# A build-time scheduler with another model of its DMA queues: DeltaNet followed by a gated MoE layer

## The chip, the cores and the metric

One core of one Trainium2 chip. The metric is the device time of a run in microseconds (us). The engines are called PE (matrix multiply), DVE (VectorE), ACT (ScalarE), POOL (GpSimd) and SP (SyncE, which issues most transfers). PE's weight loads are a row of their own, PEld.

## The reference

Inputs: q, k, v of shape (4 batches, 8 heads, 768 steps, 48), beta (4, 8, 768), w_in (384, 2048), w_out (2048, 384). q, k, v and beta are float32; the kernel gets w_in and w_out as float64 bit patterns.

```python
k_n = k / (norm(k, axis=-1) + 1e-6)
for t in range(768):                       # per batch and head
    y[t] = q[t] @ state                    # state: 48 x 48, from zero
    v_old = state.T @ k_n[t]
    state = state + beta[t] * outer(k_n[t], v[t] - v_old)
x = y.transpose(0, 2, 1, 3).reshape(3072, 384)
h = x @ w_in
out = (h * cos(h)) @ w_out                 # (3072, 384)
```

## The kernel before, in words

**Attention.** The 768 steps are cut into 24 units of 32 steps; the work of one unit covers all 4 batches and 8 heads. Two units are a pair. For unit n the tasks are, in the kernel's own names: loads of `k`, `q`, `v` (four transfers each, one for each batch; from unit 8 on other layouts with more transfers); `turn` (transposes on PE) and `turn_out` (copy by ACT); `gram` (products of keys with keys and queries: 32 small matmuls in the program, 64 in the trace, where every fp32 matmul counts twice); `gram_keys` and `gram_queries` (DVE); `gram_put` (store of the scaled products to DRAM). For each pair, `gram_get` reads them back in another layout, `inv` inverts 128 triangular 32 x 32 matrices column by column (L672 and L679; the first pair on DVE, all later ones on POOL), `put` stores the inverse to DRAM (L688) and `get` reads it back as `zt` (L697). Then, unit after unit: `state` (products with the running state, L714), `right` (DVE), `solve` (L745), `solve_out` (which makes `u`, DVE), `update` (L768) and `update_out` (new state, DVE), `within` (L785), `within_out` (copy of `y`, ACT), `features` (transpose, L804) and `features_out` (`x_ffn`, ACT). The state makes this a chain from unit to unit.

**MoE.** It runs per pair (256 tokens). The first two pairs have plain `hidden` blocks, 8 for each pair (L825, 24 matmuls in the trace), each followed by four steps of gating (`turns` ACT, `rest` DVE, `cos` ACT, `gate` DVE); the first pair also has plain output, 8 `out` groups of 8 matmuls (L970). All other products are Strassen-like: `layer` (L944), `left` and `right` sums on DVE, `product` (L1027) and `collect` (L1077). PSUM has three banks for hidden blocks (tag `h`), and one tile each for most attention products.

**Weights.** 28 `weights` tasks load 64-bit words (0 to 11 are w_in, 12 to 27 w_out) into one of eight shared tiles with the tag `g`. Each then passes `split` (two instructions on ACT), `shift` (two on DVE) and `add` (one on POOL, L488), which leave a float32 weight.

**Order.** Nothing of the order is left to the runtime. The class `Order` holds each of these tasks with an engine, a cost, a due time, what it needs and the buffers that it makes and frees. At build time `run` plays the tasks through a model of the engines: at each moment an engine takes the ready task with the earliest due time whose buffers fit; `NUDGE` shifts due times by kind of task, `STICK` keeps PE with tiles of one size, `stall` adds waits for PE's instruction blocks. The order in which the tasks are emitted is then pinned on each engine. A task that issues transfers is on SP here; in the model its transfers start when one of `IN_FLIGHT = 8` places is free. Each transfer also uses one of eight completion semaphores in turn, over all issuing engines, and the program makes the issuing engine wait for the transfer eight places ahead.

```python
end = max(end, flights[-self.IN_FLIGHT]) + self.ISSUE
dma_free = max(dma_free, end + 0.5) + moves / parts
flights.append(dma_free + 1.4)
```

On the chip each engine runs its own pinned list, and waits for semaphores where the data asks for it. The lists decide what stands behind a waiting instruction.

Of the kernel before, what the change touches and what calls it, by code (L numbers as in the profile page):

```python
# [46 lines left out]
class Order:  # L47
# [9 lines left out]
    WINDOW = 818.445  # L57
    LAG = {"PE": 0.2, "DVE": 0.15, "ACT": 0.15, "POOL": 0.2, "SP": 2.0, "IN": 0.0}
    IN_FLIGHT, ISSUE = 8, 0.49

    STEADY, LATE = 130.0, {"SP": 3.0, "POOL": 2.0}
    SLOW, WARM = 1.7, 4.0
    STICK = 1.823
    CHANGE = 0.15

    EARLY, NUDGE = 6, {('state', True): -3.4, ('features', False): -48.4, ('left', True): 37.6, ('solve', True): -19.7, ('turn', False): 12.2, ('within', True): -6.1, ('features_out', True): 39.0, ('rest', False): -12.6, ('weigh', False): -49.2, ('gram_put', True): 12.6, ('collect', False): -26.2, ('within', False): -32.5, ('features', True): -14.4, ('gate', True): -24.7, ('layer_out', False): -12.4, ('update', True): -10.5, ('sum', False): 24.3, ('layer', False): -1.8, ('add', True): -24.4, ('cos', True): 15.7, ('update', False): -6.1, ('solve', False): -34.1, ('norms', True): -9.2, ('state', False): -9.6, ('sum', True): 20.5, ('right', True): 24.7, ('hidden', True): 17.1, ('blocks', False): 2.6, ('gram', False): -8.1, ('inv_out', False): -15.0, ('v', False): 17.4, ('out', True): -13.0, ('eye', True): -0.5, ('features_out', False): -17.0, ('within_out', False): -0.6, ('gram_get', False): 12.2, ('gram_get', True): -21.0, ('turns', True): 8.1, ('scale', True): 5.8, ('k', True): -20.2, ('shift', True): -4.8, ('shift', False): 2.4, ('collect', True): 0.5, ('out', False): 0.3, ('scale', False): -1.8, ('out_out', True): 0.9, ('weigh', True): 5.0, ('store', True): -5.1, ('split', False): 9.0, ('within_out', True): -1.7, ('turns', False): -10.9, ('store_right', True): 3.6, ('turn_out', True): 1.5, ('k', False): 0.9, ('store_right', False): -5.1, ('inv', False): 5.4, ('square', False): 7.4, ('square', True): 4.1, ('norms', False): -1.3, ('store', False): 3.3, ('hidden', False): -4.1, ('cos', False): 3.4, ('x_sum', False): -0.6, ('beta_home', False): -1.9, ('store_left', True): -3.3, ('get', False): -6.1, ('get', True): 4.0, ('in_sums', False): 2.9, ('gram_queries', True): 1.6, ('turn_out', False): 5.0, ('update_out', False): -0.3, ('store_left', False): 0.1, ('inv', True): 1.1, ('v', True): -0.9, ('eye', False): -2.2, ('x_sum', True): 0.7, ('split', True): -3.1, ('beta_home', True): -4.7, ('weights', True): -0.3, ('gate', False): -3.7, ('put', False): -1.3, ('inv_out', True): -1.1, ('gram_keys', True): 0.6, ('solve_out', False): -1.5, ('add', False): 1.0, ('in_sums', True): 0.3}
# [19 lines left out]
    def add(  # L86
        self, key, engine, cost, emit, deps=(), makes=(), uses=(), moves=0.0, due=1e9
    ):

        assert key not in self.tasks, key  # L90
        self.tasks[key] = [engine, cost, due, emit, set(deps), makes, uses, moves]
        for t in uses:
            self.users[t] = self.users.get(t, 0) + 1
        for tag, t in makes:
            self.tiles[t] = tag
# [7 lines left out]

    def stall(self, key, now, commit):

        n = count = self.count(key)
# [3 lines left out]
        for i in range(self.written + 1, self.written + n + 1):  # L110
            t = now + cost * (i - self.written) / n + stall
            if (i + self.PHASE + self.AHEAD) % self.BLOCK == 0:
                there[(i + self.PHASE + self.AHEAD) // self.BLOCK + 1] = t + self.FETCH
# [135 lines left out]
def kernel(  # L249
# [32 lines left out]
    nc = tc.nc  # L282
# [1204 lines left out]
```

## Time and profile before

| what | before |
|---|---|
| three runs | 670.65, 673.01, 675.20 us; median 673.01 |
| the profiled execution | 673.73 us, its span 672.0 us |
| PE busy | 611.2 us (91% of the span), 11864 matmuls |
| DVE, POOL, ACT busy | 476.5, 347.1, 246.6 us |
| moved by DMA | 52.55 MB, of it 49.98 MB through SP's queue and 0.39 MB through ACT's |

The span runs from the first to the last instruction; the profiled execution's own time is 1.7 us longer. "Busy" rows with forty digits are the span in slices of 16.8 us, each digit a tenth. In a timeline, a line has start, length, engine, source line and operation; brackets tell how long the engine was idle ahead of it and who ended the wait. PE's busy time includes the effect of its granted clock.

### The profile page before, as it was taken

The numbers are of one execution on the slowest core, as the hardware profiler recorded it, in microseconds if no ns is written. First come the engines' busy times: TensorE is split into PE (matmuls) and PEld (weight loads), VectorE is DVE, ScalarE is ACT, GpSimd is POOL, SyncE is SP. The second block draws the span as 40 slices with busy tenths as digits, with TensorE's granted clock in tenths as the row PEclk, the third lists the DMA queues.
The fourth block names the chain that finished last, engine by engine and source line by source line (L and its number), as shares of the span: only waits on it lengthen the run. The fifth ranks groups of instructions, "written<-read, shape, count | busy, mean of one in ns | idle before, by whom it ended". The sixth has DMA issues, their size and how long they took to land.

```text
span 672.0 us, 27226 instructions
## 1 busy us (share of the span) xinstructions
PE 611.2 (91%) x11864; PEld 572.8 (85%) x11864; DVE 476.5 (71%) x913; ACT 246.6 (37%) x414; POOL 347.1 (52%) x734
## 2 busy tenths in 40 slices
PE   4303798999999999999999999999999999999997
PEld 3202687986899999999999999999999999999996
DVE  5799498977676785886876876776766666656661
ACT  4432356551133342542432433433333334333420
POOL 4369797986848428587285383482382670000000
PEclk9999798999999999999999999999999999999999
DMA  8897655465453463434524524515213202000000
GB/s 179 198 199 158 155 130 161 103 115 90 68 96 65 63 101 59 90 56 68 109 36 60 113 34 65 107 26 92 56 21 57 56 7 54 1 4 24 1 24 24
DMA packets 215515, 52.55 MB, mean 78 GB/s; under 512 B 206948, under 2 KB 210164, under 8 KB 215396
## 3 DMA queue, kind: packets, MB, share of 16 engines
q1 hardware_dynamic: 212964, 49.98, 38.6%
q8 instruction: 93, 1.52, 1.0%
q10 hardware_dynamic: 2176, 0.39, 0.4%
q0 software_dynamic: 256, 0.44, 0.3%
q14 instruction: 26, 0.21, 0.1%
HBM read 39.76 MB, written 11.01 MB: 76 GB/s over the span
## 4 chain that ended last, share of the span: by engine, by line
PE 82%; POOL 7%; DMA 4%; DVE 2%; issue 2%; ACT 1%; SPq 1%; POOLq 0%; ACTq 0%
PE p_h L944 30%; PE p_out L1027 29%; PE p_kq L714 4%; PE p_h L825 4%; PE p_out L970 3%; PE p_u L745 2%; PE p_s L768 2%; PE p_kq L785 2%; PE p_g L596 2%; POOL part L672 2%; POOL z L679 2%; DMA gb<-g_dr 2%; POOL knrm L517 2%; PE p_o L1027 2%; POOL w_in L488 1%
## 5 line engine op out<-in xcount | busy, mean ns | idle before, releaser
L672 POOL TENSOR_TENSOR part<-z,gb 128x126 f32<-128x126 f32 (+22 forms) x341 | 136.0, 399 | 106.4 <-DMA gb<-g_dr 64.2
L679 POOL TENSOR_TENSOR z<-z,part 128x126 f32<-128x126 f32 (+22 forms) x341 | 137.3, 403 | 26.7
L944 PE MATMUL p_h<-x_ffn,w_in 128*128 128x128 f32 x1120 | 143.4, 277 | 0.0
L944 PEld LDWEIGHTS p_h<-x_ffn,w_in 128*128 128x128 f32 x1120 | 135.4, 192 | 1.2
L1027 PE MATMUL p_out<-w_out,g_ffn 128*128 128x192 f32 x672 | 123.8, 329 | 1.0 <-issue 1.0
L865 ACT ACTIVATE turns<-p_h,quarter_turn 128x512 int32<-128x512 f32 x96 | 65.8, 686 | 130.4 <-DVE p_h L963 96.2
L1027 PEld LDWEIGHTS p_out<-w_out,g_ffn 128*128 128x128 f32 x672 | 107.6, 190 | 1.7 <-issue 0.5
L1027 PE MATMUL p_out<-w_sum,g_ffn 128*128 128x192 f32 x496 | 91.6, 329 | 0.0
L881 ACT ACTIVATE turns<-turns,halfpi 128x512 f32<-128x512 f32 x96 | 69.1, 721 | 46.6 <-DVE turns L872 45.9
L872 DVE SCALAR_TENSOR_TENSOR turns<-p_h,turns 128x512 f32<-128x512 f32 x96 | 65.6, 684 | 23.4 <-ACT turns L865 23.3
L1027 PEld LDWEIGHTS p_out<-w_sum,g_ffn 128*128 128x128 f32 x496 | 79.3, 190 | 0.9
L1043 DVE TENSOR_TENSOR g_ffn<-g_ffn 128x512 f32<-128x512 f32 x88 | 63.2, 719 | 13.6 <-PE p_out L1027 13.3
L517 POOL TENSOR_TENSOR knrm<-ksum,halves 128x16 f32<-128x16 f32 (+1 forms) x14 | 37.2, 2657 | 66.7 <-DVE ksum L505 66.7
L884 DVE TENSOR_TENSOR g_ffn<-turns,p_h 128x512 f32<-128x512 f32 x96 | 65.0, 679 | 7.5 <-ACT turns L881 6.6
L963 DVE TENSOR_TENSOR p_h<-g_ffn,p_h 128x512 f32<-128x512 f32 x60 | 41.7, 695 | 40.0 <-PE p_h L944 37.9
L960 ACT COPY g_ffn<-p_h 128x512 f32<-128x512 f32 x60 | 35.1, 584 | 77.7 <-PE p_h L944 77.6
L825 PE MATMUL p_h<-x_ffn,w_in 128*128 128x128 f32 x384 | 47.6, 282 | 0.7 <-POOL w_in L488 0.6
L825 PEld LDWEIGHTS p_h<-x_ffn,w_in 128*128 128x128 f32 x384 | 45.2, 196 | 2.1 <-POOL w_in L488 1.1
L1077 DVE SCALAR_TENSOR_TENSOR o<-p_out,o 128x192 f32<-128x192 f32 x74 | 25.2, 353 | 28.9 <-PE p_out L1027 27.6
L944 PE MATMUL p_h<-x_sum,in_sum 128*128 128x128 f32 x320 | 43.7, 280 | 0.0
L944 PEld LDWEIGHTS p_h<-x_sum,in_sum 128*128 128x128 f32 x320 | 39.5, 192 | 1.1
L755 DVE TENSOR_TENSOR u<-p_u,bz 128x384 f32<-128x384 f32 x48 | 24.5, 552 | 14.9 <-PE p_u L745 14.6
(95 smaller groups left out, 759.0 us busy)
## 6 DMA issues: line engine op xcount, KB each, us to landing
pairs<-in_moe_w_in_dram SPq DMA_DIRECT2D x12, 512.0 KB
gb<-g_dr SPq DMA_DIRECT2D x24, 256.0 KB
pairs<-in_moe_w_out_dram SPq DMA_DIRECT2D x16, 384.0 KB
vp<-in_v_dram SPq DMA_DIRECT2D x96, 48.0 KB
out_dram<-o SPq DMA_DIRECT2D x23, 192.0 KB
z_dr<-z SPq DMA_DIRECT2D x12, 256.0 KB
zt<-z_dr SPq DMA_DIRECT2D x96, 32.0 KB
kp<-in_k_dram SPq DMA_DIRECT2D x128, 24.0 KB
```

What stands on the lines that cost most here:

```text
L517: nc.gpsimd.tensor_tensor(out=scales[m][2][:, part], in0=sums[m, part.start][:, 0:n], in1=halves[:, 0:n], op=ALU.pow,)
L672: eng.tensor_tensor(out=part, in0=z[:, 0:rows, j, None].to_broadcast(shape), in1=a[:, j, None, j + 1 :].to_broadcast(shape), op=ALU.mult,)
L679: eng.tensor_tensor(out=behind, in0=behind, in1=part, op=ALU.subtract)
L825: nc.tensor.matmul(p_h[:, i], w_in[:, t, (4 * k + i) * 128 : (4 * k + i + 1) * 128], xts[p][:, t, unit * 128 : (unit + 1) * 128], start=(t ...
L865: nc.scalar.activation(turns[p, f], hidden_of(p, f), AF.Identity, bias=quarter_turn, scale=TURN)
L872: nc.vector.scalar_tensor_tensor(out=r, in0=hidden_of(p, f), scalar=TURN, in1=t, op0=ALU.mult, op1=ALU.subtract,)
L881: nc.scalar.activation(r, r, AF.Sin, bias=halfpi, scale=2.0 * math.pi)
L884: nc.vector.tensor_tensor(out=place(p, f), in0=step_of(rests.pop((p, f)), f), in1=step_of(hidden_of(p, f), f), op=ALU.mult,)
L944: nc.tensor.matmul(p_h[:, e], in_sum[:, odd_tile, 4 * s + e] if a == "s" else w_in[:, a, f * 128 : (f + 1) * 128], x_sums[p][:, unit] if b ...
L963: nc.vector.tensor_tensor(out=block(p, s, 0, 1) if i == 3 else p_h, in0=block(p, s, *one), in1=p_h, op=ALU.add,)
L1027: nc.tensor.matmul(p_o, left(p, part, a)[:, e % 4], right(e, b), start=(e == 0), stop=(e == FT // 2 - 1), skip_group_check=True,)
L1043: nc.vector.tensor_tensor(out=left(p, s, to), in0=left(p, s, one), in1=left(p, s, two), op=op)
```

## The change

The model behind the build-time order is changed, and with it the order on every engine; some transfers go to ACT's queue. The operations, their sizes and what they compute stay. The edits:

- **Transfers in the model.** `run` now keeps for each transfer when it begins and ends on the DMA engines, its descriptors and its issuing engine. A transfer waits for the end of the one eight places ahead (`LANES`), for the transfer before it, and for room in a ring of 128 descriptors of its own queue.
- **`ON_ACT`.** The 19 named tasks issue from ACT's queue: `weights` 0, 5, 6, 9 to 13, 15, 17 to 19, `gram_put` 2 and 5, `q` 5, `v` 2 and 3, `put` 0 and `get` 1. The emitting functions ask `queue(...)` for the engine. With the four transfers of `q`, `v` and `get` that is 31 transfers.
- **`HOLD`.** 48 named tasks may not start in the model before a given time. This acts at build time alone; the program has no such wait.
- **Numbers.** `WINDOW`, `LATE`, `STICK`, `CHANGE`, the due times of weights (`W_IN`, `W_OUT`, `LOADS`), `START`, `FIRST`, `STEP`, many task costs, and `NUDGE`, which can now name a single task too. A block of PE instructions is taken to arrive 1.5 us later in the first 130 us.

```diff
-    WINDOW = 818.445
+    WINDOW = 949.811
...
-    IN_FLIGHT, ISSUE = 8, 0.49
-    STEADY, LATE = 130.0, {"SP": 3.0, "POOL": 2.0}
+    RING, ISSUE, LANES = 128, 0.49, 8
+    DESCRIPTORS = {
+        "weights": 8, "gram_put": 64, "gram_get": 4, "put": 128, "blocks": 32, "store": 8,
+        "store_left": 8, "store_right": 8,
+    }
+    STEADY, LATE = 130.0, {'SP': 1.64, 'POOL': 0.17, 'DVE': 1.1, 'ACT': 0.25}
...
-    STICK = 1.823
-    CHANGE = 0.15
+    STICK = 10.881
+    CHANGE = 0.17
...
+        if key in self.ON_ACT:
+            assert moves
+            engine = "ACT"
...
+    def descriptors(self, key):
+        n = self.DESCRIPTORS.get(key[0], 16)
+        if key[0] in ("k", "gram_put") and key[1] >= 8:
+            n //= 2
+        return n
...
-            task[2] += self.NUDGE.get((key[0], n < self.EARLY), 0.0)
+            task[2] += self.NUDGE.get((key[0], n < self.EARLY), 0.0) + self.NUDGE.get(key, 0.0)
...
-                able = [x for x in heap if x[0] <= limit and fits(x[2])]
+                able = [
+                    x for x in heap
+                    if x[0] <= limit and fits(x[2]) and self.HOLD.get(x[2], 0.0) <= now
+                ]
...
-                        end = max(end, flights[-self.IN_FLIGHT]) + self.ISSUE
-                        dma_free = max(dma_free, end + 0.5) + moves / parts
-                        flights.append(dma_free + 1.4)
-                    done = flights[-1]
+                        end = max(end, accepted.get(engine, 0.0), flights[-self.LANES][1] + 1.1)
+                        begin = max(flights[-1][1], end + 0.95)
+                        flights.append(
+                            (begin, begin + moves / parts, self.descriptors(key), engine)
+                        )
+                        accepted[engine], room = end + 0.3, self.RING
+                        for a, b, n, on in reversed(flights):
...
+                            room -= n
+                        end += self.ISSUE
+                    done = flights[-1][1] + 1.4
...
+    def queue(*key):
+        return nc.scalar if key in Order.ON_ACT else nc.sync
...
-        nc.sync.dma_start(out=words[t], in_=src)
+        queue("weights", t).dma_start(out=words[t], in_=src)
...
-    W_IN, W_OUT, LOADS = 24.824, 4.888, 290.255
+    W_IN, W_OUT, LOADS = -14.976, -122.868, 481.274
...
-    START = 41.528
-    FIRST, STEP = 2.12, 3.854
+    START = 21.924
+    FIRST, STEP = 2.979, 3.897
...
-        add(("cos", *key), "ACT", 1.45, lambda: hidden_cos(p, f), [("rest", *key)])
+        add(("cos", *key), "ACT", 0.75, lambda: hidden_cos(p, f), [("rest", *key)])
```

**What stands where, after.** PE's list begins with turns 0 and 1, grams 0 and 1, turns 2 and 3, grams 2 and 3, turn 4, solve 0, update 0, within 0, features 0, state 1, two hidden blocks, solve 1; before, gram 4 stood ahead of state 1 and no hidden block ahead of solve 1. On SP, `get` 0 stands behind `q` 7, and `get` 2 and 3 directly behind `put` 1 and one `gram_put`. On ACT, `put` 0 stands behind the split of weight 7, then the split of weight 8, the load of weight 9, four loads of `v` 3, the split of weight 9, the load of weight 10 and `get` 1. On DVE the shift of weight 9 stands ahead of `solve_out` 0.

## The prediction

> **What bounds the kernel now.** I read the slices of the page first: TensorE (PE) is full everywhere except in the first seven slices, and there the DMA row is at its highest.
>
> ```profile
> span 672.0 us, 27226 instructions
> PE   4303798999999999999999999999999999999997
> DMA  8897655465453463434524524515213202000000
> ```
>
> Then the table by stage, in two divisions, to see how much idle time there is and where. Its columns: stretch, its length, busy us of PE, of PE's weight loads, of VectorE (DVE), ScalarE (ACT) and GpSimd (POOL), each with its instructions, the granted clock, the DMA share and GB/s.
>
> ```profile
> 16.80:33.60 16.80, 5.32 (x140) 4.17 (x140) 13.08 (x43) 7.37 (x14) 6.41 (x5) 1.00 0.88 198
> 33.60:50.40 16.80, 1.08 (x4) 0.71 (x4) 15.43 (x48) 6.05 (x10) 10.44 (x25) 1.00 0.93 200
> 50.40:67.20 16.80, 5.51 (x208) 5.03 (x210) 15.59 (x25) 4.55 (x8) 15.78 (x19) 1.00 0.74 158
> 67.20:84.00 16.80, 12.14 (x298) 11.14 (x287) 8.10 (x15) 5.89 (x12) 12.93 (x28) 0.80 0.66 155
> ...
> 97.00:117.50 20.50, 18.38 (x386) 15.21 (x388) 16.04 (x36) 11.00 (x21) 15.11 (x27) 0.92 0.60 164
> 117.50:154.30 36.80, 36.80 (x660) 33.55 (x661) 31.19 (x54) 19.56 (x35) 28.99 (x50) 1.00 0.57 117
> 154.30:646.00 491.70, 490.53 (x9579) 465.14 (x9579) 345.06 (x631) 174.72 (x285) 236.85 (x564) 1.00 0.32 56
> ```
>
> PE is idle 672.0 - 611.2 = 60.8 us. From 117.5 to 646 it is idle 1.2 us, in the tail 4.9. The remaining 54.7 us lie before 117.5, and only these can be won by order alone. Everything from 117.5 on is a rigid block of PE work: it starts earlier or later and keeps its length.
>
> Third, the waits of PE and the timelines of PE and SP for that stretch.
>
> ```profile
> PE p_u L745 <- DMA zt<-z_dr: 25.4, 1, 25.4
> ...
> 60.49 1.94 PE L745 MATMUL p_u<-vp,zt 32*32 32x48 f32 x64 [25.38 <-DMA zt<-z_dr]
> 74.59 1.50 PE L745 MATMUL p_u<-rhs,zt 32*32 32x48 f32 x64 [2.37 <-issue]
> 94.56 2.75 PE L970 MATMUL p_out<-w_out,g_ffn 128*128 128x384 f32 x8
> 113.69 3.81 PE L970 MATMUL p_out<-w_out,g_ffn 128*128 128x384 f32 x8
> ...
> 48.22 0.39 SPq L688 DMA_DIRECT2D z_dr<-z  x1
> 48.70 5.04 SPq L369 DMA_DIRECT2D qp<-in_q_dram  x4
> 55.82 0.39 SPq L465 DMA_DIRECT2D pairs<-in_moe_w_in_dram  x1
> 56.26 4.24 SPq L697 DMA_DIRECT2D zt<-z_dr  x8
> ```
>
> The first solve (60.49) waits for the first inverse to go to DRAM and back. The store is issued at 48.22; then SP issues other loads, one group of four of them held for 5.04 us instead of 1.9, and only at 56.26 the load that reads the inverse back.
>
> **What the skill says.** (1) The Trainium skill, "DMA: Bandwidth & Descriptors", section "Issuing engines are not separate DMA queues": issuing from several engines saves only issue time, since all run on the same 16 DMA engines. Before has only eight early loads on ACT, so its trace doesn't test it; but with the DMA share at 0.85 to 0.93 until 50 us I expect no bandwidth from the second queue. (2) Same page, section "Anatomy of one DMA": a wait for a semaphore is held on the issuing sequencer before dispatch. The 5.04 us line above agrees. On ACT such a wait would hold the activations behind it. (3) "TensorE: Matmul & The Clock Gate", section "What's actually happening": after an idle window PE runs at half clock until it has been busy a few us. Agrees: the 24 matmuls of one hidden block took 4.01 us at 76.02 and 2.68 us later. (4) "GPSIMD Engine Reference", section "Key points": GpSimd shares its SBUF interfaces with VectorE. Agrees: one weight add took 1.28 us at 17.40 and three took 5.10 at 49.38 beside a busy DVE.
>
> **The change, part by part.** No operation is added or removed: both programs have 6000 matmul rows. What changes is the order on each engine, and that 31 transfers after the start go to ACT's queue. I compare the two orders at a point with the same set of PE work before it: the end of the second output group of the first pair (L970, 113.69 + 3.73 = 117.42). In both orders 7 turns, 6 grams, 3 solves, updates, withins, features and states, 7 hidden blocks and 2 output groups precede it. All times to come are worked out from durations of the trace of before.
>
> *First solve.* Up to the gram stores the orders cost the same (one weight load goes to ACT, but the key norms still take 1.66 us each on POOL), so the inverse on DVE still starts at 27.5 and ends at 45.8. The store of it is now on ACT, behind the split of weight 7, which landed at 47.0: 48.3, no earlier than before. But the read-back is the next thing that SP does once the store has landed: 3.8 us (the gram stores, issued until 19.0, released their reader at 22.79), so issue from 52.5, and as in before the data is there with the last of the four issues or little later: 56.5. DVE must do five weight shifts (1.4 each), small work of 1.4 and the weighing of v (2.03) after 45.8: 56.2. Bytes: by 60 us before moved 11.31 MB at 188 GB/s; after needs about 10.7 MB for this: 57. I take 57.0, with 55 and 60.5 as bounds.
>
> *To the second solve.* On DVE the shift of weight 9 stands ahead of the first u. Weight 9 is issued by ACT after the split of weight 8 (53.4), lands 4.4 later, and ACT first issues four loads of v: split 59.2, shift 60.6, u 61.8, update 63.4, within 64.9 (still at cold durations, 1.56 and 1.50), features 66.4, state 68.0. Then two hidden blocks are ahead of solve 1; the second needs weight 4, whose add is on POOL behind the first 16 columns of inverse 1 (39 to 59.6 with two adds inside), four adds (65.6), a root (3.44) and the add of weight 10: 71.8. So hidden 68 to 72 and 72 to 75, solve 1 at 75.0 against 74.59. It looks like nothing gained, but PE has done two hidden blocks more and one gram less: 6.8 - 1.2 = 5.6 in cold durations, less the 0.4. Lead about 5 us.
>
> *To the first output group.* It needs weights 12 to 15. POOL: four columns (76.1), weights 11 and 12 (78.6), twelve columns (9.6, from 63.5 to 78.7 less the add, scaled to these columns) to 88.2, three adds of 1.02: 91.2. PE has hidden 3 and 4, update, turn, within, gram, state and features done at 87.7: it waits 3.5 us, and ends the group at 91.9. Before ended it at 97.23 with one gram (0.8) more: lead 4.5.
>
> *To the comparison point.* The second inverse is stored at 88.7 and read back at once (before: store 80.72, read-back held until 90.07): solve 2 at 96.0 against 97.23, with a hidden block more done. Before then loses 0.28 + 0.91 + 0.93 us to waits and 1.2 to a clock dip (3.81 against 2.58 for the output group). After I find one wait, 1.2 us for ACT's copy of y, and the second output group ends at 110.6. Lead 117.42 - 110.6 = 6.8.
>
> *Rest.* The last weight add comes near 145 in after, and the fourth output group wants it near 144: -0.9. From there PE is full, as before. Switching into small tiles and out again costs 0.2 us (an output group of eight takes 1.50 after them and before them, 1.30 otherwise); the orders make 86 and 82 such excursions: +0.8. The tail is the same chain of products. Sum: 6.8 - 0.9 + 0.8 = 6.7 us. The profiled execution took 673.73, span 672.0 within it; 673.7 - 6.7 = 667.0. The median of the runs shown is 0.7 lower, 673.01: **666.3 us**.
>
> The edits of planner costs, dues and nudges have no price of their own; they act through the order that I read. The 31 ACT issues at 0.49 us are 15 us of ACT, which is 37% busy: nothing while none waits, and what a waiting one costs is rival three.
>
> **Rivals.** *The bytes decide* (0.18): for it speaks the DMA share above and that the store isn't earlier; the first solve stays at 60.5 and the lead shrinks to the reordering, 2 to 3 us: 670.5. Against it: the DMA share falls to 0.74 from 50 to 67, while SP held transfers in an unlucky order. *More than forecast* (0.10): the first solve at 55, weights 12 to 15 not late (3.5): 6.7 + 2 + 3.5 = 12.2, so 661. For it: POOL's durations beside a quieter DVE can be a quarter shorter. *ACT as issuer is held* (0.22, the slower side): each of the transfers on ACT waits for the one eight places ahead, and splits, copies of y and cosines stand behind it; DVE's u stands behind a shift that needs the split. SP's 47 transfers of 26.4 to 55.8 took 0.62 us each against 0.48 unheld, and the worst four 1.26 each. At that worst price, 0.8 more for each of the 18 transfers between 45 and 95 us, the chain loses 14 us: 6.7 - 14 = -7.5, so 681. It decides from a hold of 0.4 us each (slower from 673) and for over 1% from 0.75. Against: most ACT transfers are single weights with a split of slack. That the change doesn't do what it says isn't a rival: the order shows the read-backs directly behind the stores and 19 keys on ACT.
>
> **Chances and range.** Forecast 0.50, of which about 0.30 falls past 1% and 0.20 within (its own span is 662 to 670); bytes 0.18 (0.15 within, 0.03 slower by noise and small holds); more 0.10; held 0.22. Within 1% is about what a measurement of this kernel can tell from no change (the three runs span 4.5 us). Faster 0.40, same 0.35, slower 0.25. Range 659 to 680.
>
> **What would show it.** Right: first solve at 55 to 59, solve 1 near 75 with two hidden blocks before it, the second L970 group ending at 108 to 113, PE full after it, 82 excursions. Wrong: a first solve at 60 or later; ACT idle ahead of its own DMA issues for more than 1 us several times; DVE's u behind a shift that waits for ACT; new PE waits of over 3 us after 150 us.

## The result, and the profile after

The changed kernel took 676.07 us (median of 20 runs, 674.4 to 680.42), the kernel before 673.05 us in the same comparison (20 runs, 668.64 to 677.28). The ratio is 1.0053 (95% interval 1.0038 to 1.0069): 3 to 4 us slower, a small loss that the interval tells from no change. Forecast was a gain of 6.7 us.

The profiled execution of the changed kernel took 674.67 us, only 0.9 more than the profiled one of before. So the pair of profiles shows less than the medians do, and part of the work below is to find out why. First the page of after: its span, and PE and DMA in 40 slices.

```profile
span 672.9 us, 27161 instructions
PE   3312989998999999999999999999999999999997
DMA  8886556483454353534443533514410402000000
```

The fourth to sixth digit of PE were 3, 7, 9 before and are 2, 9, 8 now. After that both rows are nearly full. The table by stage of after (columns as in the prediction):

```profile
0.00:60.16 60.16, 13.63 (x297) 11.36 (x297) 40.91 (x130) 21.78 (x39) 29.50 (x48) 0.70 0.85 190
60.16:111.90 51.74, 44.18 (x1193) 38.74 (x1194) 44.37 (x75) 25.39 (x46) 44.75 (x61) 0.85 0.57 138
111.90:154.00 42.10, 39.65 (x670) 34.58 (x668) 33.34 (x59) 23.77 (x43) 34.83 (x63) 1.00 0.66 133
154.00:646.00 492.00, 489.40 (x9578) 465.09 (x9579) 342.34 (x631) 172.00 (x284) 238.61 (x564) 1.00 0.32 56
```

The third line is new: 2.45 us of PE's time are idle where before had none (its line from 117.5 to 154.3 read 36.80 of 36.80). In the fourth line PE is idle 2.6 us, before 1.2.

The timeline of after, PE's lines:

```profile
60.16 1.70 PE L785 MATMUL p_u<-vp,zt 32*32 32x48 f32 x64 [19.64 <-issue]
64.84 1.56 PE L808 MATMUL p_s<-u,kp 64*64 64x96 f32 x32 [2.98 <-DVE u L795]
...
77.37 0.88 PE L785 MATMUL p_u<-rhs,zt 32*32 32x48 f32 x64
...
92.13 4.44 PE L1010 MATMUL p_out<-w_out,g_ffn 128*128 128x384 f32 x8
100.27 0.88 PE L785 MATMUL p_u<-rhs,zt 32*32 32x48 f32 x64
...
111.90 2.75 PE L1010 MATMUL p_out<-w_out,g_ffn 128*128 128x384 f32 x8
...
149.31 2.75 PE L1010 MATMUL p_out<-w_out,g_ffn 128*128 128x384 f32 x8
153.96 2.85 PE L1010 MATMUL p_out<-w_out,g_ffn 128*128 128x384 f32 x8 [1.90 <-ACT o L1022]
```

Line numbers are those of the changed kernel, 40 higher than before's for the same code. The first solve starts at 60.16, not at 57; the first output group takes 4.44 us instead of the 2.75 of before; the second ends at 114.6, not at 110.6; and two output groups now stand next to each other (149.31 and 153.96), with PE idle until ACT has copied the first one's bank.

Why the first solve is late is in the timelines of SP, ACT and DVE of the same execution:

```profile
43.52 4.56 SPq L409 DMA_DIRECT2D qp<-in_q_dram  x4
48.44 2.01 SPq L409 DMA_DIRECT2D kp<-in_k_dram  x4
50.56 0.39 SPq L505 DMA_DIRECT2D pairs<-in_moe_w_in_dram  x1
...
54.86 0.66 ACT L513 ACTIVATE w_in<-pairs 128x512 f32<-128x512 f32 x1 [5.51 <-DMA pairs<-in_moe_w_in_dram]
...
56.12 0.78 DVE L519 SCALAR_TENSOR_TENSOR pairs<-pairs 128x512 uint32<-128x512 uint32 x1 [4.01 <-ACT pairs L515]
...
58.77 1.18 DVE L593 TENSOR_TENSOR vp<-vp,knrm 128x768 f32<-128x768 f32 x1
```

SP is held at the load of q 6 (4.56 us for four transfers that take 1.9 unheld), so weight 8 is issued only at 50.56. ACT waits 5.51 us for it, DVE 4.01 us for ACT's split, and the weighing of v (L593), which the first solve needs, stands behind that shift and ends at 59.95.

### The profile page after: what moved, and what is told of

Its sections match the earlier page's. It is cut to its first block, busy times and chain, and to the rows that moved or that the text cites. A ratio compares the mean times of both kernels' runs of the same rounds, so it can differ in the third digit from the quotient of the medians.

```text
span 672.9 us, 27161 instructions
## 1 busy us (share of the span) xinstructions
PE 608.5 (90%) x11864; PEld 570.8 (85%) x11864; DVE 471.4 (70%) x913; ACT 244.7 (36%) x414; POOL 347.7 (52%) x734
## 4 chain that ended last, share of the span: by engine, by line
PE 76%; POOL 10%; DMA 7%; issue 2%; DVE 2%; SPq 1%; ACT 1%; POOLq 0%; ACTq 0%; DVEq 0%
PE p_h L984 30%; PE p_out L1067 29%; PE p_kq L754 4%; POOL part L712 4%; POOL z L719 4%; PE p_s L808 3%; PE p_kq L825 2%; PE p_u L785 2%; PE p_g L636 2%; POOL w_out L528 2%; DMA pairs<-in_moe_w_in_dram 2%; PE p_out L1010 2%; DMA kp<-in_k_dram 2%; PE p_o L1067 2%; DMA qp<-in_q_dram 1%
## 5 line engine op out<-in xcount | busy, mean ns | idle before, releaser
L719 POOL TENSOR_TENSOR z<-z,part 128x126 f32<-128x126 f32 (+22 forms) x341 | 138.8, 407 | 26.7
L1067 PE MATMUL p_out<-w_out,g_ffn 128*128 128x192 f32 x672 | 122.0, 329 | 0.5 <-DVE o L1117 0.5
L1067 PE MATMUL p_out<-w_sum,g_ffn 128*128 128x192 f32 x496 | 88.6, 329 | 0.0
L921 ACT ACTIVATE turns<-turns,halfpi 128x512 f32<-128x512 f32 x96 | 68.8, 721 | 39.7 <-DVE turns L912 38.6
L1083 DVE TENSOR_TENSOR g_ffn<-g_ffn 128x512 f32<-128x512 f32 x88 | 61.9, 704 | 19.9 <-PE p_out L1067 18.4
L1003 DVE TENSOR_TENSOR p_h<-g_ffn,p_h 128x512 f32<-128x512 f32 x60 | 41.7, 696 | 42.3 <-PE p_h L984 37.6
L984 PE MATMUL p_h<-x_sum,in_sum 128*128 128x128 f32 x320 | 42.0, 277 | 0.0
L754 PE MATMUL p_kq<-st,kq_t 48*32 48x48 f32 x2944 | 33.2, 215 | 3.2 <-issue 3.2
```

Of the source, the lines that this page charges most:

```text
L719: eng.tensor_tensor(out=behind, in0=behind, in1=part, op=ALU.subtract)
L754: nc.tensor.matmul(p_kq[quarter(b), par, a, j], kq_t[rows48(par), a, b * NP + j], st[rows48(par), b // 2, j, b % 2], start=(j == 0 and a = ...
L921: nc.scalar.activation(r, r, AF.Sin, bias=halfpi, scale=2.0 * math.pi)
L984: nc.tensor.matmul(p_h[:, e], in_sum[:, odd_tile, 4 * s + e] if a == "s" else w_in[:, a, f * 128 : (f + 1) * 128], x_sums[p][:, unit] if b ...
L1003: nc.vector.tensor_tensor(out=block(p, s, 0, 1) if i == 3 else p_h, in0=block(p, s, *one), in1=p_h, op=ALU.add,)
L1067: nc.tensor.matmul(p_o, left(p, part, a)[:, e % 4], right(e, b), start=(e == 0), stop=(e == FT // 2 - 1), skip_group_check=True,)
```

## The experiments

For all of them the order was written out: `run` emits a fixed list of the 1870 tasks, the one that the planner gives for before or for after, or parts of both, with single tasks moved. With a list left as it was, the instructions of each engine stand exactly as in the kernel it was taken from.

```diff
     def run(self, wrote):
-        ...
+        for key in FROZEN:
+            self.tasks[key][3]()
+            wrote([tag for tag, _ in self.tasks[key][5]])
```

For the readings the span is cut where both orders have the same set of PE work behind them: at the end of the second output group of the plain pair (point A) and at the end of the fifth (point B). The table has the profiled executions; all times in us. "First solve" and "second solve" are the starts of their first matmuls. Where the read-back landed in parts most of the first solve ran later: it had its last part at 58.2 in the new order on SP, 60.5 in "the same, again", 62.6 and 60.1 in the two kernels with moves, 64.0 with the early eight back, 65.5 with the weights alone and 59.2 with the read-back first. A profiled execution can also lie off the median of its kernel: "weights alone" and "moves at the first solve" were the slowest of six each, 3.2 and 1.9 us above theirs.

| kernel | first solve | second solve | point A | A to B | B to PE's end | PE idle after B |
|---|---|---|---|---|---|---|
| before | 60.5 | 74.6 | 117.5 | 39.4 | 510.2 | 1.2 |
| before, again | 59.1 | 73.7 | 111.8 | 39.8 | 510.4 | 1.4 |
| after | 60.2 | 77.4 | 114.6 | 42.2 | 511.3 | 3.1 |
| after, again | 58.8 | 77.7 | 116.3 | 41.1 | 511.0 | 3.0 |
| new order, all on SP | 57.2 | 73.9 | 113.1 | 42.6 | 510.1 | 2.0 |
| old order, 19 tasks on ACT | 59.0 | 71.8 | 111.7 | 39.4 | 511.3 | 1.8 |
| the same, again | 59.3 | 73.1 | 111.2 | 40.1 | 510.2 | 1.2 |
| new start, old rest | 59.7 | 77.3 | 114.2 | 42.3 | 510.6 | 1.2 |
| old start, new rest | 59.5 | 73.0 | 115.2 | 39.4 | 512.6 | 4.3 |
| new until A, then old | 59.7 | 79.1 | 116.0 | 41.9 | 510.8 | 1.4 |
| moves at the first solve | 59.5 | 80.2 | 116.1 | 43.9 | 511.3 | 3.2 |
| moves at the first solve, old from A | 57.0 | 78.0 | 114.6 | 42.0 | 511.5 | 2.2 |
| groups apart | 60.1 | 77.6 | 115.2 | 39.9 | 511.7 | 3.7 |
| groups apart, old rest | 60.5 | 76.9 | 116.9 | 40.2 | 511.6 | 2.3 |
| early eight back on SP | 59.6 | 79.9 | 118.0 | 42.0 | 510.3 | 2.5 |
| old order, weights alone on ACT | 63.2 | 77.2 | 120.1 | 40.7 | 509.6 | 0.9 |
| old order, ACT, read-back first | 55.8 | 74.3 | 113.4 | 39.6 | 509.1 | 0.4 |
| old order, ACT, u first | 58.4 | 70.5 | 113.3 | 39.4 | 510.0 | 1.2 |

**Order alone, queue alone.** The diff has two parts that can be separated: where the tasks stand, and which engine issues 19 of them.

```diff
 # the order of after, order_only
-ON_ACT = {('weights', 18): 1, ...}
+ON_ACT = {}
```

> The order of the changed kernel, emitted from a written list, with all 31 transfers put back on SP's queue. Theory A (what the time was lost to is the order: a first solve held by the late split of weight 8, output groups that wait for ACT's copy, a denser pattern of short waits after 150 us): the ratio to the kernel before stays where the changed kernel has it or goes higher, 1.003 to 1.012 (675 to 681 us), with the first solve at 60 to 63 us, since 19 more issues stand in SP's line, and the wait ahead of the third output group at 150 us still there. Rival B (issuing from ACT is what costs): the ratio falls below 1.001 and ACT's own work in the first 110 us ends earlier.

Measured 1.0051 (1.0035 to 1.0066). The order loses as much without the other queue as the changed kernel does in its first comparison; rival B falls. But the guess that the first solve would come later was wrong: with all transfers on SP it began at 57.2, the value that the prediction had for the changed kernel. How far apart two comparisons can be is seen below, where the changed kernel itself measured 1.0093; differences of 0.2% between kernels from different comparisons are not read here.

```diff
 # the order of before, queue_only
-ON_ACT = {}
+ON_ACT = {('weights', 18): 1, ...}   # the 19 of the change
```

> The order of the kernel before, emitted from a written list, with the changed kernel's 19 tasks issued by ACT. Theory A: the rest after 150 us is that of the kernel before to the instruction, so the ratio lies within 0.998 to 1.004 (the start may move by -1 to +3 us by what ACT holds); waits of PE after 150 us sum to 1.2 us as before. Rival B: ACT held by its issues delays the copies and splits, the second output group ends at 119 us or later (before 117.4) and the ratio is 1.004 or more.

> The order of the kernel before with the 19 tasks on ACT once more, for what its gain is worth: ratio 0.995 to 0.998 if it is real; 0.999 or more if the first comparison was luck. Second group at 111 to 113.5 us against 114 to 117.5 of the kernel before.

Measured 0.9963 (0.9948 to 0.9979), and 0.9966 (0.9951 to 0.9982) the second time. So the queue by itself makes the kernel before 0.35% faster, more than theory A had allowed, and this is the version that beats both kernels. By the table its gain lies before point A. What comes earlier there can be followed, first in the kernel with the old start on SP alone (the "new rest" kernel; timelines of SP, POOL and PE):

```profile
97.12 1.09 SPq L683 DMA_DIRECT2D gb<-g_dr  x2
...
102.91 0.24 POOL L712 TENSOR_TENSOR part<-z,gb 128x31 f32<-128x31 f32 x1 [4.49 <-DMA gb<-g_dr]
...
110.75 1.99 POOL L528 TENSOR_TENSOR w_out<-w_out,pairs 128x384 uint32<-128x384 uint32 x2
...
109.95 0.66 PE L605 MATMUL p_t<-consts,kp 128*128 128x128 f32 x4 [0.88 <-ACT x_ffn L852]
111.99 0.66 PE L605 MATMUL p_t<-consts,qp 128*128 128x128 f32 x4 [1.38 <-issue]
112.48 2.75 PE L1010 MATMUL p_out<-w_out,g_ffn 128*128 128x384 f32 x8
```

and then with the queue:

```profile
92.77 1.09 SPq L683 DMA_DIRECT2D gb<-g_dr  x2
...
99.01 0.24 POOL L712 TENSOR_TENSOR part<-z,gb 128x31 f32<-128x31 f32 x1 [1.05 <-DMA gb<-g_dr]
...
106.98 2.00 POOL L528 TENSOR_TENSOR w_out<-w_out,pairs 128x384 uint32<-128x384 uint32 x2
...
108.94 2.75 PE L1010 MATMUL p_out<-w_out,g_ffn 128*128 128x384 f32 x8
```

With the put of Gram block 5 and several weights gone from SP's line (weight 17 is issued at 91.42 instead of 96.63), the read-back of the Gram blocks of pair 2 is issued 4.4 us earlier, and POOL begins that pair's inverse when it has landed. The last two adds for the second output group stand behind columns of this inverse: from its first column to their end it takes 9.8 us without the queue and 10.0 with it, and 9.3 to 10.1 in all eight profiles of the old start. By these profiles it is this trip, and not the issue of weight 17, that lets the adds end at 109.0 instead of 112.7. The group ends 3.5 us earlier. PE waited for these adds in neither kernel, though: without the queue it waited 0.88 us for ACT's copy of `x_ffn` and 1.38 us for nothing that the profile shows, with it not at all from 96 us to the group. Which of these links decides is not shown. (In one of three profiles the old start without the queue got to point A as early, at 111.8; with the queue both did.)

**Which half of the run.** After exactly 432 tasks both orders have emitted the same set. So the halves can be exchanged.

```diff
 # new_start:  AFTER[:432] + BEFORE[432:], queue as after
 # new_rest:   BEFORE[:432] + AFTER[432:], all on SP
```

> The changed kernel's order and queues up to the point where exactly the same 432 tasks are emitted in both kernels (about 156 us on the chip), and the order of the kernel before from there on. Theory A, with a loss of about 2 us in the profile after 154 us: the ratio falls to 0.997 to 1.001, PE's waits after 156 us sum to 1.2 us again. Rival C (the start costs time that the one profile of the changed kernel didn't show): the ratio stays at 1.004 to 1.007.

> The mirror image: the order and the queue of the kernel before for the first 432 tasks, the changed kernel's order from there on. Theory A: slower by what the rest loses, ratio 1.003 to 1.007, with the pattern of short waits (0.3 to 0.6 us each) after 156 us as in the changed kernel. Rival C: 0.999 to 1.001.

Measured 1.0058 (1.0036 to 1.0079) and 1.0033 (1.0015 to 1.0051). Both lose. The second is as theory A had it, and its idle time after B is 4.3 us. The first went against theory A: with before's rest PE's waits fell to 1.2 us as expected, but the ratio stayed where the changed kernel's was. So the first 156 us lose too, where the profile pair showed a lead; which half loses more the two intervals don't tell.

**Both kernels once more.**

> The changed kernel itself once more, for a second profile beside the same runs of before as the others. If the gap of 2 us between the profile pair (0.9 us) and the medians (3.0 us) is that the profiled execution of before had a late start (second group at 117.5 us against 115.2 in a second profile of the same instructions): ratio 1.004 to 1.007 again, second group at 114 to 116, from there to the fifth group 42.2 us, the rest 510 to 511.5. If it is a loss that one profile doesn't show, one of these three is over 1 us longer.

> The kernel before itself, for a second profile of it and for the noise of the comparison: ratio 0.998 to 1.002. If its first profile (second output group at 117.5 us) was a late execution, this one has it at 114 to 116 us, with 39.4 us to the fifth group and 510 to 511 us from there to the end; if that was its usual start, at 117 or later.

Measured 1.0093 (1.0069 to 1.0117; six runs) and 1.0011 (0.9994 to 1.0028). The ratio of the changed kernel came out above what was expected, and the new start of before, at 111.8, lay in neither of the places expected. They show what the profile pair hid. The start of before is not one number: its instructions reached point A at 117.5 us in the profile of the prediction, at 115.2 in "old start, new rest" and at 111.8 in this execution. The line that starts the second output group in the new profile of before:

```profile
109.05 2.75 PE L970 MATMUL p_out<-w_out,g_ffn 128*128 128x384 f32 x8
```

It was at 113.69 in the profile that the prediction used, the latest of the three. The new start with its queue, unchanged up to A, was profiled six times: 114.2 to 116.9, mean 115.5, against 114.8 for the three of before. Against the medians of their own runs the profile of before was 0.7 us late, that of after 1.4 early; the new profile of before was 3.7 early. The lead of 2.8 us in the profile pair was in good part this accident.

**The output groups back to back.** First the order of before was put in from point A on:

```diff
 # mid_before:  AFTER[:294], then the rest in the order of BEFORE, queue as after
```

> The changed kernel's order and queues up to the end of the second output group of the plain pair (the task sets of both kernels are equal there on TensorE), then the order of the kernel before. Theory A (the output groups put back to back, which wait for ACT's copy, cost 2.9 us between the second group and the fifth): second group ends at 114 to 115 us as in the changed kernel, the fifth ends 39.3 us later instead of 42.1 to 42.5, ratio 0.999 to 1.003, 2.9 us or 0.4% under the 1.0058 of the kernel that takes the order of before only from 156 us on. Rival (the wait only shows a delay that comes back elsewhere, or the loss is not in these 40 us): the ratio stays at 1.004 to 1.007.

Measured 1.0058 (1.0032 to 1.0084): the rival held. The wait for ACT's copy is gone, but A to B is 41.9 us all the same. The timeline of this kernel shows the wait that took its place:

```profile
111.76 1.01 POOL L528 TENSOR_TENSOR w_out<-w_out,pairs 128x384 uint32<-128x384 uint32 x1
121.15 1.13 POOL L528 TENSOR_TENSOR w_out<-w_out,pairs 128x384 uint32<-128x384 uint32 x1
...
131.82 2.10 PE L1010 MATMUL p_out<-w_out,g_ffn 128*128 128x384 f32 x6
135.06 0.91 PE L1010 MATMUL p_out<-w_out,g_ffn 128*128 128x384 f32 x2 [1.14 <-POOL w_out L528]
```

The new order has two parts of an inverse on POOL between the adds of weights 19 and 20 (111.76 and 121.15), before's has one. So the third group's weights come late, and the new order had used its hidden blocks up ahead of that group; none was left to stand between the fourth and the fifth. The other way to mend it stays inside the new order:

```diff
 # groups_apart: the order of after, with
-POOL ... norms 5, add 27 ...
+POOL ... add 27, norms 5 ...
-PE   ... hidden 1 14, out 0 0 3, out 0 1 0 ...
+PE   ... out 0 0 3, hidden 1 14, out 0 1 0 ...
-ACT  ... turns 1 14, ..., out_out 0 0 ...
+ACT  ... out_out 0 0, turns 1 14 ...
```

> The changed kernel with four moves around 145 to 155 us and nothing else: the last weight's add ahead of the root of pair 5 on POOL, the fourth output group ahead of the last hidden block on TensorE instead of behind it, and its copy ahead of that block's turns on ACT. Theory A2 (the changed kernel has spent its hidden blocks early, since its weights come later on POOL, so that the fourth and fifth groups stand back to back and the fifth waits for the fourth's copy): the wait of 1.90 to 2.03 us for ACT goes, the time from the second group's end to the fifth's falls from 42.2 to 40 to 40.3 us, ratio 1.002 to 1.0035. Rival (as in the run that took over the order of before there: another wait, for a weight's add, takes its place): 41.5 us or more, ratio 1.0045 to 1.006.

```profile
147.17 2.75 PE L1010 MATMUL p_out<-w_out,g_ffn 128*128 128x384 f32 x8
149.75 2.84 PE L865 MATMUL p_h<-x_ffn,w_in 128*128 128x128 f32 x24
152.43 2.75 PE L1010 MATMUL p_out<-w_out,g_ffn 128*128 128x384 f32 x8
```

In its timeline the hidden block stands between the groups and PE doesn't wait for the copy; A to B fell to 39.9 us, as expected (42.2 and 41.1 in the two profiles of after). Measured 1.0058 (1.0039 to 1.0078): by itself this ratio lies where the rival had it. But the unchanged kernel beside it stood at 1.0093, and against that the gain is 1.9 us, as large as expected (medians of 673.58 and 675.49 us, over nine and six runs). With before's rest as well:

```diff
 # apart_before_rest: groups_apart[:432] + BEFORE[432:]
```

> The changed kernel with the fourth and fifth output groups apart (as in the run that did this alone) and the order of the kernel before from 156 us on, where the task sets are equal. What is left of the change is its start and its queue. If the start gives nothing against the usual start of the kernel before: ratio 0.999 to 1.003, second group at 114 to 116, 39.9 us to the fifth, PE's waits after it 0.4 to 1.8 us. If the start gives the 2.8 us that the profile pair shows: 0.995 to 0.998. If the start itself loses, beyond what the profiles show: 1.004 or more.

Measured 1.0033 (1.0018 to 1.0048), between the cases "gives nothing" and "loses". What is left of the change, mainly its start, gains nothing and may cost 1 to 2.4 us: its median is 673.41 us, that of before in the same comparison 671.00, and of before run once more beside it 672.31.

**The first solve.** Here the chain in after's profile was taken at its word: weight 8 first, the weighing ahead of its shift.

```diff
 # weight8_first: the order of after, with
-SP   ... q 6, k 6, weights 8 ...
+SP   ... weights 8, q 6, k 6 ...
-DVE  ... shift 8, shift 7, weigh 0, sum 2, shift 9, solve_out 0 ...
+DVE  ... weigh 0, shift 8, shift 7, solve_out 0, sum 2, shift 9 ...
 # mended: these moves up to point A, then the order of before
```

> The changed kernel with four moves: the load of weight 8 is issued ahead of the q load of unit 6 on SP, weigh 0 stands ahead of the shifts of weights 8 and 7 on DVE, and the shift of weight 9 and the row sum of pair 2 stand behind the first u. Theory A (the first solve is held by weigh 0, that by the shift behind the late split of weight 8): first solve at 57 to 58 us instead of 60.2, first u 2 us earlier still, second output group ends at 111 to 113 instead of 114.7, ratio 1.000 to 1.003. Rival (the transfers ahead of the read-back decide, so that another of them becomes last): first solve at 59.5 us or later, ratio 1.004 to 1.007.

> Both edits together: the four moves at the first solve, and the order of the kernel before from the second output group on. Theory A: the two gains add, second group at 111 to 113, fifth 39.3 us later, ratio 0.994 to 1.000. Rivals: 1.001 or more, if one of the two gains is taken back by a wait that takes its place.

Measured 1.0082 (1.0050 to 1.0113) and 1.0067 (1.0039 to 1.0096): theory A failed in both, and the first ratio lies above its rival too. The timeline of the second, DVE and PE:

```profile
50.98 1.15 DVE L593 TENSOR_TENSOR vp<-vp,knrm 128x768 f32<-128x768 f32 x1
...
56.99 0.33 PE L785 MATMUL p_u<-vp,zt 32*32 32x48 f32 x2 [17.49 <-DMA zt<-z_dr]
57.79 0.61 PE L785 MATMUL p_u<-vp,zt 32*32 32x48 f32 x4 [0.47 <-DMA zt<-z_dr]
60.05 1.48 PE L785 MATMUL p_u<-vp,zt 32*32 32x48 f32 x58 [1.65 <-DMA zt<-z_dr]
...
70.10 7.98 PE L865 MATMUL p_h<-x_ffn,w_in 128*128 128x128 f32 x48
```

The weighing now ends at 52.1, almost 8 us earlier, and the first solve does start at 56.99. But the read-back lands in four parts, the last at 60.05, and the solve ends at 61.5 against 61.9 in after. With the weighing out of the way the last landing is the limit, and only 0.3 us are won. Then the two hidden blocks ahead of the second solve, the first that PE runs after its long idle time, took 7.98 us here and 6.3 in after.

```diff
 # late_on_act: the order of after, with
-ON_ACT = {weights 0, 5, 6, 9, q 5, v 2, v 3, gram_put 2, ...}
+ON_ACT = {...}   # the other eleven
```

> The changed kernel's order with eleven of its 19 tasks on ACT: the eight that ACT issues before or at the first inverse's put and weigh (weights 0, 5, 6, 9, q 5, v 2, v 3, the second Gram put) are back on SP. Theory G (ACT's early issues take the lanes ahead of SP's loads of q 6, k 6 and weight 8, on which weigh 0 hangs through DVE's line): first solve at 57 to 58.5 us as with all on SP, weight 8 issued by 48 us instead of 50.6, second group at 111 to 113.5, ratio 1.001 to 1.005. Rival (it is put 0 or the later weights on ACT that hold the start): first solve at 59.5 or later, ratio 1.005 to 1.009.

Measured 1.0103 (1.0077 to 1.0130), slower than either expectation. A lane in the expectation is one of the eight semaphores that all transfers use in turn. Theory G was right on weight 8 (issued at 48.27) and wrong on the rest.

```profile
56.96 5.61 SPq L737 DMA_DIRECT2D zt<-z_dr  x4
...
63.99 1.49 PE L785 MATMUL p_u<-vp,zt 32*32 32x48 f32 x58 [1.16 <-DMA zt<-z_dr]
```

With more transfers on SP ahead of it the read-back itself is held, for 5.61 us, and the solve gets its last part at 63.99.

**What the queue gains on the old order.** Three variants of the queue with the order of before:

```diff
 # weights_on_act: only the 12 weight loads on ACT
 # get_first: all 19 on ACT, on SP
-SP   ... q 6, get 0 ...
+SP   ... get 0, q 6 ...
 # u_first: 18 on ACT (get 1 on SP), on DVE
-DVE  ... shift 9, solve_out 0 ...
+DVE  ... solve_out 0, shift 9 ...
```

> The order of the kernel before with only the 12 weight loads of the changed kernel's 19 tasks issued by ACT; the loads of v and q, the trips of Gram blocks and inverse and the read-back of unit 1 stay on SP. Theory D (the gain of the queue is that the weights for the second output group are issued 3 to 5 us earlier, because SP's line no longer holds them behind its own transfers): second group ends at 111 to 112.5 us as with all 19, ratio 0.995 to 0.998. Theory E (it is the put of the first inverse and the early trips that gain): second group at 114 to 115.5, ratio 0.999 to 1.001.

> The kernel before's order with the changed kernel's 19 tasks on ACT's queue, and one move: the q load of unit 6 (used at 108 us) is issued behind the read-back of the first inverse instead of ahead of it, where SP held it for 5.67 us. Theory A (in the start each transfer that stands held ahead of the read-back is late work for the first solve): first solve at 56 to 57.5 us against 59.0, second output group ends at 109.5 to 111 against 111.7, ratio 0.992 to 0.996. Rival (weigh 0, the weights or u are last as soon as the read-back is earlier): first solve 58.5 or later, or the lead gone by the second output group; ratio 0.996 to 0.998 as without the move.

> The order of the kernel before with 18 of the 19 tasks on ACT (the read-back for unit 1 stays on SP, so ACT is not held 4 to 5.7 us by its four transfers ahead of the split of weight 9), and the first u on DVE ahead of weight 9's shift. Theory D (weights for the second group decide the end of the start): the first update comes at 61 to 62 us instead of 63.2, but the second group still ends at 111 to 112.5, ratio 0.995 to 0.998. Theory F (the hold of ACT and the chain of solves decide): 109.5 to 110.5, ratio 0.992 to 0.995.

The weights alone lose: 1.0069 (1.0046 to 1.0092). Theory D falls in this form, and the timeline shows how.

```profile
50.60 4.58 SPq L409 DMA_DIRECT2D qp<-in_q_dram  x4
55.23 4.13 SPq L409 DMA_DIRECT2D vp<-in_v_dram  x4
59.41 5.80 SPq L737 DMA_DIRECT2D zt<-z_dr  x8
...
65.48 1.48 PE L785 MATMUL p_u<-vp,zt 32*32 32x48 f32 x58 [1.53 <-DMA zt<-z_dr]
...
118.21 1.88 PE L1010 MATMUL p_out<-w_out,g_ffn 128*128 128x384 f32 x4 [2.46 <-POOL w_out L528]
```

With v 3 back on SP the read-back is issued at 59.41 instead of 54.56 (old order with all 19). The read-back of the Gram blocks of pair 2 is late as well (issued at 102.68; POOL stood idle 8.1 us for it), and here PE does wait for the adds, 2.46 us. This execution was 3.2 us above its kernel's median, so its times overstate the loss. The 12 weights alone are not what gains; which of the other seven tasks the gain needs is not shown.

The other two are no better than the queue alone: 0.9972 (0.9955 to 0.9988) and 0.9980 (0.9962 to 0.9998). In the first the solve starts at 55.8, but its last part lands at 59.2, and the gain is gone at the second solve; its timeline shows ACT held by its own transfer:

```profile
54.77 5.66 ACTq L737 DMA_DIRECT2D zt<-z_dr  x4
60.48 0.68 ACT L513 ACTIVATE w_in<-pairs 128x512 f32<-128x512 f32 x1 [5.17 <-DMA zt<-z_dr]
```

The split of weight 9 stands 5.17 us behind four parts of a read-back. In the second (u first) that is gone, and the second solve comes at 70.5, the earliest of all; still point A is at 113.3, later than without the two moves. Theory F falls: in this execution the chain of solves doesn't set point A.

## Why the prediction was wrong, point by point

- **The comparison point: 117.42 against 110.6, lead 6.8.** This is the step that failed first, on both sides. 117.42 was one execution of a start that takes 111.8 to 117.5; before's usual point A is nearer 115. And after's is 114.2 to 116.9 instead of 110.6. The lead is -0.7 us by the means (115.5 against 114.8), and 0 if each profile is shifted by its distance from its own median; the spread of before's start alone is nearly as large as the lead that was forecast. A time worked out mostly from unheld durations was subtracted from a measured one that contained all its accidents.
- **First solve at 57.0.** It was at 58.8 to 60.5 in six profiles of this start. The read-back was issued at 53.27 (predicted 52.5), so that part was right. Missed were the hold of q 6 on SP and with it the late weight 8: five shifts were counted at 1.4 us each, none with a wait, and DVE lost 4.01 us to one; DVE's inverse also ended at 47.5 instead of 45.8. The rival "the bytes decide" had the number, a first solve at 60.5, but by luck: the same order with all transfers on SP began it at 57.2. The rates were alike, 190 GB/s up to the first solve of after and 187 in before; over the first 57 us the new order moved 200 GB/s with all transfers on SP and 189 and 198 with the queue. That agrees with the Trainium skill, "DMA: Bandwidth & Descriptors", section "Issuing engines are not separate DMA queues": two issuers brought no bandwidth here.
- **Second solve at 75.0.** 76.9 to 79.1. In the profile of after, the first update started at 64.84 instead of 63.4, since PE waited 2.98 us for u, which stood behind the shift of weight 9; the prediction listed just this among the signs that it is wrong. The hidden blocks began at 71.1 instead of 68 and took 6.3 us instead of 7.
- **First output group ends at 91.9.** 96.6 in after. The adds of weights 12 to 15 were set at 91.2 and ended at 94.6. But the group ended 2 us after them, with no wait in it: its matmuls were slow, 4.44 us for all eight, at a clock recorded as 0.62.

```profile
92.10:96.60 4.50, 4.50 (x22) 2.18 (x28) 3.75 (x5) 1.65 (x4) 4.50 (x4) 0.62 0.93 182
```

In the kernel "groups apart, old rest" the clock stayed at 1.00 and the group waited for its adds instead (0.79 us in three waits). In the other nine profiles with the new start the group took 3.48 to 5.02 us, in all eight with the old start 2.75. Ahead of it PE had been idle for 1.9 to 3.5 us of the last 8 in the new start, for 0.0 to 1.3 in the old. The prediction had the 3.5 us of waiting there, but a warm group behind it; this term was put at nothing, and makes the group 0.7 to 2.3 us longer. How much of that reaches point A stays open.
- **Fourth output group: -0.9.** The place was right and the size was not. A to B took 42.3 us (mean of the six profiles with the new order unchanged in this stretch) against 39.7 (mean of the eight with the old order on both sides of A): -2.6 us. The last add was set near 145 and came at 150.7, behind a root of 3.21 us on POOL; and the prediction didn't ask what is left to stand between this group and the next one.
- **Fewer small-tile excursions: +0.8.** The saving is there: from B to the end, less its waits, PE needs 508.1 us with the new rest (mean of seven) and 509.1 with the old (mean of eleven). But the new rest waits 3.1 us instead of 1.4. Together 511.2 against 510.5: -0.7. "PE is full, as before" was the false sentence; short waits of 0.3 to 0.6 us belong to an order too.
- **Sum.** -0.7 - 2.6 - 0.7 = -4.0 us. The two ratios of the changed kernel, 1.0053 and 1.0093, stand for 3.6 and 6.2 us. The terms are means over few executions; the first is known to about 2 us. That the sum agrees with the first ratio to 0.4 us is partly luck.
- **The rivals.** "ACT as issuer is held" has the right sign and the wrong cause: the order alone loses as much with all transfers on SP. The 28 ACT issues between 30 and 112 us in after took 0.42 us each, but a hold stands between two issues: the four loads of v 3 went out at 55.38, 55.81, 59.28 and 59.64, and the split of weight 9, whose own load had landed at 59.26, stood behind them until 60.15. That hold cost this split 0.9 us. A longer one is shown in another kernel (5.66 us above), which is still faster than before. That the changed order loses by itself, without any queue, was no rival at all.

Open: why the queue gains 2 to 3 us in the start of the old order and nothing in the new one. With the new order all on SP point A came at 113.1, but that execution was the fastest of its 15, 2.5 us under their median, so the order alone isn't shown to have an earlier start either. The experiments at the first solve show several limits within 3 us of each other there (the weighing, the last part of the read-back, u, the cold hidden blocks, the weights), and no single one that decides. Open too is how much of the start the slow first output group costs; no kernel here takes it away with the rest left as it is.

## What to carry to other kernels

Profile the kernel before at least twice before subtracting from it: here, where transfers of many kinds run into each other, point A of one program came at 111.8 and at 117.5 us, while the full stretch from B on repeated within 0.2 us (510.2 and 510.4). When an order is changed, ask at each stage what is left to stand between two dependent neighbours, and count the short waits that an old order has already lost. Where an order leaves PE waiting, price the matmuls behind the wait as well as the wait. A change of two parts is worth taking apart: here one part alone took 0.35% off the time of the old order, and nothing off that of the new one.

## What the runs showed of the hardware

- The mean clock of a run says little on the time of this kernel. In the profile of after it is 0.70 up to the first solve (the table above), in that of before 1.00. But the same matmuls took the same time in both: the first update 1.56 us, at a recorded 0.50 in after and at 1.00 in before, where the later ones took 0.89. So this record is no measure of the clock in the start. From 64 to 67 us, after and then before; and two updates of before:

```profile
64.00:67.00 3.00, 2.16 (x68) 1.96 (x71) 1.07 (x3) 1.25 (x2) 3.00 (x3) 0.50 0.26 39
64.00:67.00 3.00, 3.00 (x129) 2.66 (x123) 2.62 (x6) 1.88 (x3) 2.57 (x6) 1.00 0.57 94
...
63.63 1.56 PE L768 MATMUL p_s<-u,kp 64*64 64x96 f32 x32 [1.21 <-DVE u L755]
83.78 0.89 PE L768 MATMUL p_s<-u,kp 64*64 64x96 f32 x32 [0.19 <-ACT kq_t L575]
```

A lower clock as the cause of the loss is a rival that the runs speak against. All runs of kernels with the old start have a mean clock above 0.98; of 20 runs of after, 13 are below, with a median of 676.9 us, and 7 above, with 675.6. In the same order on SP it is the other way round: ten below with 674.9, five above with 676.4.
- At one place the clock does cost time: the first output group of the new start, slow at a recorded 0.62 after PE had waited (shown above). An idle time of that size does not always do it: ahead of the second group of "old start, new rest" PE was idle for 2.25 of the last 8 us, and the group took 2.75 us.
- The first hidden block after PE's long idle time took 3.65 us in one execution of after and 5.11 in another, the second one 2.84. Over all profiles, of different kernels, it took 3.40 to 5.67 us, so about 2 us of the start vary here without any edit at that place; 5.67 is twice 2.84. The Trainium skill, "TensorE: Matmul & The Clock Gate", section "What's actually happening", has a cause that fits (PE runs at half clock until it has been busy for a few us) and says that this varies from run to run; over the blocks of 3.65 and 5.11 us the recorded clock was 0.86 and 0.59.
- A transfer of four parts is not one landing. In the kernel with the early eight on SP the solve went on in steps at 59.63, 60.64, 62.47 and 63.99, as the parts of one read-back came in.
